# Eight of the row-layout heads moved to a key layout with split exponentials

## The chip, the cores and the metric

The kernel runs on one core of a Trainium2 chip. The core has a matrix engine (PE, with its weight loads shown apart as PEld), a vector engine (DVE), a scalar engine (ACT), a general engine (POOL) and a queue engine (SP) that here issues nearly all DMAs. Sixteen DMA engines serve all queues. Each engine takes its own instructions strictly in the order in which they stand; between engines there are only semaphores. The metric is the device time of one execution in microseconds.

## The reference

Two parts follow each other. The attention part hashes queries and keys into buckets, lets a query see only the keys of its own bucket, and takes a softmax over them. The second part mixes the attended rows over positions and gates them.

```python
def _attn_ref(q, k, v, proj):                 # q, k, v: 4 x 8 x 768 x 64
    q_bits = (np.einsum('bhsd,dk->bhsk', q, proj) > 0)   # 6 bits per row
    k_bits = (np.einsum('bhsd,dk->bhsk', k, proj) > 0)
    mask = q_bucket[:, :, :, None] == k_bucket[:, :, None, :]
    scores = np.where(mask, scale * np.matmul(q, k.transpose(0, 1, 3, 2)), -1e9)
    attn = np.exp(scores - np.max(scores, axis=-1, keepdims=True))
    attn = attn / (np.sum(attn, axis=-1, keepdims=True) + 1e-9)
    return np.matmul(attn, v)

def _moe_ref(x, w_in, w_spatial, b_spatial, w_out):      # x: 4 x 768 x 512
    h = np.maximum(x @ w_in, 0.0)                        # 1024 wide: u, v
    v_n = (v - mean(v)) / np.sqrt(var(v) + 1e-6)
    v_s = np.einsum('ts,bsd->btd', w_spatial, v_n) + b_spatial[None, :, None]
    return (u * v_s) @ w_out
```

## The kernel before

There are 32 heads (4 batches of 8), two to a pair, and each head is worked in 6 steps of 128 rows. A step is named g = 6n + i for head n and tile i. Every large product is done in 16-bit pieces: a number is split into a high and a low half and three of the four partial products are summed.

**Row layout** (head 0 and heads 8 to 31, function `scores`). Step i takes 128 queries as rows and all 768 keys as columns. PE makes the scores in a PSUM tile `sp` by four matmuls (lines 291 and 292). DVE reads `sp` and takes the row minimum of the negated scores into `nb` (line 293, it also writes a throw-away tile `jk`, and a small second instruction reads the accumulated value out). ACT reads `sp` again and makes the exponentials `ex` with `nb` as bias (line 295). ACT casts them to 16 bit, the high half of `pp` (line 298). DVE subtracts to get the low half (line 299); for tile 2, and for tiles 0 and 3 of heads below 16, POOL does that. The product with V needs the keys on the partitions, so SP issues a DMA transpose `pt<-pp` of both halves (line 301). Five steps later (`LAG`), `weighted` multiplies `pt` with the halves of V by 18 small matmuls (lines 314 to 316).

**Key layout** (heads 1 to 7, set `KEYS`). Step i takes 128 keys as rows and all queries as columns, so exponentials come out with the keys on the partitions and no transpose is needed. A row maximum cannot be taken there, so it is made first: `row_max` computes the masked scores of 128 queries by two matmuls into a tile `mp` (line 241), DVE reduces it (line 243), and after the sixth tile the maxima are cast (line 248), transposed by PE (line 251), copied (line 253) and written by a small DMA on SP as one more row into the operand `ab` (line 254). `scores_k` then makes scores that have the maximum in them already (lines 262 and 263), and ACT makes the exponentials as 32-bit numbers (line 265), which `weighted_k` multiplies three steps later (`LAGK`) with the 32-bit V (line 275). The row maxima of head n are made one per step from g = 6n - 10 to 6n - 5 (`LEAD`).

**Buffers.** `sp` and `mp` share two PSUM buffers (`ps_sc`). `ex` has 3 buffers, `pp` 3 (`PB`), and `pt` 5 (`PTB`); the 32-bit exponentials of the key layout take `pt` buffers too.

**What stands beside it.** Loads, the splitting of q and k (`hl`) and the building of `ab` for head n + 2 go along with the steps. The gating part of a batch is 28 units of 12 or 18 matmuls each (lines 361, 402, 417, 432), handed out at 28 units per 48 steps once the last pair of the batch is done, so that it fills PE while the next batch's heads run; the units of the last batch come after the last head. A scheduler orders each engine's instructions by a priority (`at(g, k)`) and its own estimate of readiness; the order is fixed when the program is built.

SP's queue is in order too: a transpose that waits for its `pp`, or for a `pt` buffer that `weighted` has yet to give back, holds up every load behind it.

## Time and profile before

| | us |
|---|---|
| median of 3 runs | 736.97 |
| runs | 735.91, 736.97, 740.86 |
| span of the profiled execution | 741.7 |
| from the start to the first exponential of head 8 | 174.9 |
| heads 8 to 31 | 174.9 to 655 |
| what is left of the gating part | 655 to 741.7 |

The page gives no other time for the profiled execution than its span; the span is 4.7 us over the median of the runs and 0.8 us over the highest. In the tables below, an idle time "<- X" is time in which the engine stood still until X released it. Busy times of PE have modelled ends, so they are an upper bound of what PE does.

### The profile page before, as it was taken

Reading aid. Unit: us, or ns where it says so; the run is one execution under the profiler, and the core shown is the slowest. Engines: PE = TensorE matmul, PEld = TensorE weight load, DVE = VectorE, ACT = ScalarE, POOL = GpSimd, SP = SyncE. Lnnn points to the kernel's source line nnn. Section 1 sums busy time; section 2 is a strip of 40 time slices with the busy share of each in tenths; the row PEclk is TensorE's granted clock in tenths of the full one; section 3 lists DMA queues with packets and bytes.
Section 4 is the critical chain, followed back from the end, with each engine's and each line's share of the span. In section 5 each row is a group of like instructions: output and inputs, shape, how many; then the busy total and the mean of one; then the engine's idle time right before and its main releaser. Section 6 shows DMA issues by size and latency. Waiting matters only on the chain.

```text
span 741.7 us, 14927 instructions
## 1 busy us (share of the span) xinstructions
PE 631.5 (85%) x5759; PEld 400.4 (54%) x5759; DVE 520.6 (70%) x945; ACT 434.8 (59%) x668; POOL 321.2 (43%) x324
## 2 busy tenths in 40 slices
PE   1569898998988776997898899889898998999997
PEld 0237686776445444554544555556455565654553
DVE  4677795536799999567689798678698987755200
ACT  1344574346788676655676577667677776743221
POOL 5122443123458675264314565156235571451503
PEclk9768797999999989898999999999999999999999
DMA  9565554324999989996999799999999999860011
GB/s 235 149 123 155 133 148 102 99 55 97 224 237 197 215 207 187 213 178 138 234 202 199 138 210 213 211 211 212 206 210 181 194 175 213 182 136 15 1 42 43
DMA packets 290011, 120.95 MB, mean 163 GB/s; under 512 B 270740, under 2 KB 273812, under 8 KB 289940
## 3 DMA queue, kind: packets, MB, share of 16 engines
q1 hardware_dynamic: 287636, 119.11, 76.4%
q10 hardware_dynamic: 2304, 0.89, 0.5%
q8 instruction: 45, 0.74, 0.4%
q14 instruction: 26, 0.21, 0.1%
HBM read 28.33 MB, written 6.29 MB: 47 GB/s over the span
## 4 chain that ended last, share of the span: by engine, by line
PE 43%; DMA 21%; DVE 13%; issue 8%; ACT 6%; POOL 6%; SPq 3%; ACTq 0%; DVEq 0%; POOLq 0%
DMA pt<-pp 14%; PE pv L275 6%; PE vps L361 6%; PE ops L432 5%; PE sps L417 5%; PE ups L402 5%; DMA ab<-hl 4%; PE sp L291 3%; DVE jk L293 3%; PE sp L292 3%; DVE pp L299 2%; PE sp L262 2%; PE pv L314 2%; ACT ex L295 2%; PE sp L263 2%
## 5 line engine op out<-in xcount | busy, mean ns | idle before, releaser
L295 ACT ACTIVATE ex<-sp,nb 128x768 f32<-128x768 f32 x150 | 134.1, 897 | 54.8 <-DVE jk L293 48.9
L299 DVE TENSOR_TENSOR pp<-ex,pp 128x768 f16<-128x768 f32 x116 | 126.2, 1089 | 47.6 <-ACT pp L298 46.5
L293 DVE TENSOR_SCALAR_CACHE_REDUCE jk<-sp 128x768 bf16<-128x768 f32 x150 | 142.4, 949 | 24.1 <-PE sp L292 22.2
L298 ACT CAST pp<-ex 128x768 f16<-128x768 f32 x150 | 124.3, 829 | 50.0 <-DMA pt<-pp 43.9
L314 PE MATMUL pv<-vp,pt 128*128 128x65 f16 x900 | 108.2, 198 | 40.5 <-DMA pt<-pp 40.2
L291 PE MATMUL sp<-ab 128*128 128x384 f16 x300 | 103.2, 344 | 31.6 <-ACT ex L295 19.3
L314 PEld LDWEIGHTS <-pt 128*128 128x128 f16 x900 | 86.7, 101 | 67.2 <-DMA pt<-pp 53.4
L299 POOL TENSOR_TENSOR pp<-ex,pp 128x768 f16<-128x768 f32 x34 | 58.1, 1708 | 131.1 <-ACT pp L298 124.6
L315 PE MATMUL pv<-vp,pt 128*128 128x64 f16 x900 | 108.0, 197 | 0.0
L316 PE MATMUL pv<-vp,pt 128*128 128x65 f16 x900 | 107.8, 198 | 0.0
L292 PE MATMUL sp<-ab 127*128 127x384 f16 x300 | 103.9, 346 | 0.0
L417 PE MATMUL sps<-ws,vn 128*128 128x384 f16 x576 | 100.9, 329 | 1.5 <-DVE sg L180 1.0
L315 PEld LDWEIGHTS <-pt 128*128 128x128 f16 x900 | 87.0, 100 | 11.3 <-issue 1.3
L316 PEld LDWEIGHTS <-pt 128*128 128x128 f16 x900 | 86.9, 100 | 3.1 <-issue 0.5
L417 PEld LDWEIGHTS <-vn 128*128 128x128 f16 x576 | 55.3, 99 | 37.8 <-issue 3.9
L432 PE MATMUL ops<-wo,g 128*128 128x512 f16 x288 | 70.9, 391 | 1.5 <-ACT o L436 0.9
L275 PEld LDWEIGHTS pv<-vf,ex 128*128 128x128 f32 x504 | 68.5, 208 | 4.1 <-issue 1.6
L402 PE MATMUL ups<-xt,wi 128*128 128x384 f16 x384 | 69.1, 333 | 1.3 <-ACT u L405 0.9
L361 PE MATMUL vps<-wi,xt 128*128 128x512 f16 x288 | 68.0, 383 | 1.4 <-DMA xt<-xs 1.3
L275 PE MATMUL pv<-vf,ex 128*128 128x65 f32 x504 | 67.0, 286 | 0.0
L333 POOL TENSOR_TENSOR x<-x,xf 128x384 f32<-128x384 f32 x32 | 35.5, 1110 | 64.1 <-DVE x L332 64.1
L422 POOL TENSOR_TENSOR sy<-sy,u 128x384 f32<-128x384 f32 x32 | 36.6, 1145 | 49.3 <-DVE sy L421 49.2
(87 smaller groups left out, 1010.7 us busy)
## 6 DMA issues: line engine op xcount, KB each, us to landing
qk<-kq SPq DMA_DIRECT2D x16, 768.0 KB
ab<-hl SPq DMA_DIRECT2D x31, 384.0 KB
ab<-hl SPq DMA_DIRECT2D x34, 192.0 KB
out<-o SPq DMA_DIRECT2D x24, 256.0 KB
v<-v SPq DMA_DIRECT2D x13, 384.0 KB
raw<-w_in SPq DMA_DIRECT2D x16, 256.0 KB
pt<-pp SPq DMA_TRANSPOSE x150
raw<-w_sp SPq DMA_DIRECT2D x12, 192.0 KB
```

What stands on the lines that cost most here:

```text
L275: nc.tensor.matmul(acc[:, qi, :], lhsT=ex[:, qi * P:(qi + 1) * P], rhs=vf[p % 2][:, 2 * i + e, :], start=(i == 0 and qi == 0), stop=(i == ...
L291: nc.tensor.matmul(ps[:, c], lhsT=t[:, 0, qs], rhs=t[:, 1, cs], start=True, stop=False)
L292: nc.tensor.matmul(ps[:, c], lhsT=t[0:P - 1, 3, qs], rhs=t[0:P - 1, 2, cs], start=False, stop=True)
L293: nc.vector.tensor_scalar(jk, ps, -ISQ, None, op0=ALU.mult, op1=ALU.min, accum_out=nb)
L295: st["ex", n, i] = nc.scalar.activation(ex, ps, AF.Exp, bias=nb, scale=ISQ).ins
L298: nc.scalar.copy(pp[:, 0], ex)
L299: (nc.gpsimd if i in (PL_POOL if n >= 2 * NH else PL_POOL1) else nc.vector).tensor_tensor(out=pp[:, 1], in0=ex, in1=pp[:, 0], op=ALU.subtract)
L314: nc.tensor.matmul(acc, lhsT=pt[:, c, :], rhs=vh, start=(i == 0 and c == 0), stop=False)
L315: nc.tensor.matmul(acc[:, 0:D], lhsT=pt[:, c, :], rhs=vl, start=False, stop=False)
L316: nc.tensor.matmul(acc, lhsT=pt[:, NT + c, :], rhs=vh, start=False, stop=(i == NT - 1 and c == NT - 1))
L361: nc.tensor.matmul(ps, lhsT=xt[c][:, gx, i * P:(i + 1) * P], rhs=wi[gw][:, c, F2:DF], start=(k == 0), stop=(k == 3 * NPAIR - 1))
L417: nc.tensor.matmul(ps[:, :HS], lhsT=vn[gv][:, c, d * P:(d + 1) * P], rhs=ws[gw][:, c, hs], start=(k == 0), stop=(k == 3 * NT - 1))
```

## The change

Heads 10, 13, 16, 19, 22, 25, 28 and 31 leave the row layout. They get row maxima ahead of time like heads 1 to 7, and scores by `scores_k`. Unlike those, their exponentials are split into 16-bit halves by ACT and DVE, the halves lie in a `pt` buffer (tile `pk`), and `weighted_k` multiplies them with the 16-bit halves of V, again by 18 small matmuls. All six subtractions of such a head are DVE's, none is POOL's.

```diff
     def has_keys(p):
-        return 2 * p in KEYS or 2 * p + 1 in KEYS
+        return 2 * p in KF32 or 2 * p + 1 in KF32
...
@@ scores_k
+        if n in KSPLIT:
+            pp = wk.tile([P, 2, 2, HS], F16, tag="pt", bufs=PTB, name=f"pk{n}_{i}")
+            ex = wk.tile([P, 2, HS], F32, tag="ex", bufs=EB, name=f"ex{n}_{i}")
+            st["ex", n, i] = nc.scalar.activation(ex, ps, AF.Exp, scale=ISQ).ins
+            nc.scalar.copy(pp[:, 0], ex)
+            nc.vector.tensor_tensor(out=pp[:, 1], in0=ex, in1=pp[:, 0], op=ALU.subtract)
+            st["pt", n, i] = pp
+            return
...
@@ weighted_k
+        if n in KSPLIT:
+            pk = ex.rearrange("p g c q -> p g (c q)")
+            vl, vh = vp[p % 2][:, 2 * i + e, 0:D], vp[p % 2][:, 2 * i + e, D:2 * D + 1]
+            for qi in range(NT):
+                qs = slice(qi * P, (qi + 1) * P)
+                nc.tensor.matmul(acc[:, qi, :], lhsT=pk[:, 0, qs], rhs=vh, start=(i == 0 and qi == 0), stop=False)
+                nc.tensor.matmul(acc[:, qi, 0:D], lhsT=pk[:, 0, qs], rhs=vl, start=False, stop=False)
+                nc.tensor.matmul(acc[:, qi, :], lhsT=pk[:, 1, qs], rhs=vh, start=False, stop=(i == NT - 1 and qi == NT - 1))
+            return
...
-    KEYS = {1, 2, 3, 4, 5, 6, 7}
+    KF32 = {1, 2, 3, 4, 5, 6, 7}
+    KSPLIT = {10, 13, 16, 19, 22, 25, 28, 31}
+    KEYS = KF32 | KSPLIT
```

The order of instructions changes at two kinds of places. In the names below the first number after the letters is the head (of `hl`, `xs`, `xt`, `v32` and `qk`: the pair), the second the tile, the last one a serial number.

DVE, around the second step of head 18, before the change. `jk` is the minimum, `pp` the subtraction, the others belong to the gating part:

```order
L299 TENSOR_TENSOR pp18_0_4592<-ex18_0_4590,pp18_0_4592 128x768
L293 TENSOR_SCALAR jk18_1_4639,nb18_4582<-sp18_1_4640 128x768
L370 BN_AGGR mv1_0_4272<-bs1_2_4459 128x2
L339 TENSOR_TENSOR xs8_4525<-x16_4522,xs8_4525 128x6x64
L369 BN_STATS bs1_3_4544<-vr1_3_4541 128x6
L293 TENSOR_SCALAR jk18_2_4671,nb18_4582<-sp18_2_4672 128x768
L377 TENSOR_SCALAR ve1_0_4462<-mv1_0_4272 128x3
L370 BN_AGGR mv1_3_4543<-bs1_3_4544 128x2
L299 TENSOR_TENSOR pp18_1_4648<-ex18_1_4646,pp18_1_4648 128x768
```

The same engine at the same place now; `mx19` are reductions for head 19, which is one of the eight:

```order
L243 TENSOR_REDUCE mx19_4444<-mp19_3_4601 128x1
L310 TENSOR_SCALAR jk18_0_4627,nb18_4626<-sp18_0_4628 128x768
L316 TENSOR_TENSOR pp17_5_4596<-ex17_5_4594,pp17_5_4596 128x768
L386 BN_STATS bs1_4_4684<-vr1_4_4682 128x6
L243 TENSOR_REDUCE mx19_4444<-mp19_4_4641 128x1
L405 TENSOR_SCALAR vy1_2_4546<-vr1_2_4525,mv1_0_4335,rs1_0_4532 128x512
L387 BN_AGGR mv1_3_4583<-bs1_4_4684 128x2
L310 TENSOR_SCALAR jk18_1_4687,nb18_4626<-sp18_1_4688 128x768
L316 TENSOR_TENSOR pp18_0_4636<-ex18_0_4634,pp18_0_4636 128x768
L243 TENSOR_REDUCE mx19_4444<-mp19_5_4701 128x1
```

Between two minima of heads 17 and 18 there now stands one more full-width reduction, and each `mp` that it reads takes one of the two PSUM buffers that the `sp` tiles use.

SP, from the end of head 18 through head 19, before the change:

```order
L344 DMA_TRANSPOSE xt8_4833<-xs8_4525 128x12x128
L301 DMA_TRANSPOSE pt18_5_4847<-pp18_5_4844 128x12x128
L301 DMA_TRANSPOSE pt19_0_4906<-pp19_0_4903 128x12x128
L211 DMA ab1_83<-hl10_4422 64x2x1536
L212 DMA ab1_83<-hl10_4422 64x1536
L301 DMA_TRANSPOSE pt19_1_4944<-pp19_1_4941 128x12x128
L158 DMA v32_11_4946<-v 128x768
L301 DMA_TRANSPOSE pt19_2_4992<-pp19_2_4989 128x12x128
L301 DMA_TRANSPOSE pt19_3_5033<-pp19_3_5030 128x12x128
L301 DMA_TRANSPOSE pt19_4_5083<-pp19_4_5080 128x12x128
L301 DMA_TRANSPOSE pt19_5_5155<-pp19_5_5152 128x12x128
L152 DMA qk12_5157<-kq 128x1536
```

SP now, from the second step of head 18 to the first of head 20:

```order
L318 DMA_TRANSPOSE pt18_1_4699<-pp18_1_4696 128x12x128
L254 DMA ab3_85<-mt19_4711 1x6x128
L361 DMA_TRANSPOSE xt8_4894<-xs8_4487 128x12x128
L318 DMA_TRANSPOSE pt18_2_4744<-pp18_2_4741 128x12x128
L318 DMA_TRANSPOSE pt18_3_4814<-pp18_3_4811 128x12x128
L318 DMA_TRANSPOSE pt18_4_4861<-pp18_4_4858 128x12x128
L158 DMA v32_11_4998<-v 128x768
L318 DMA_TRANSPOSE pt18_5_4908<-pp18_5_4905 128x12x128
L152 DMA qk12_5230<-kq 128x1536
L318 DMA_TRANSPOSE pt20_0_5263<-pp20_0_5260 128x12x128
```

Head 19's six transposes are gone, and the small write of its maxima (`ab3_85<-mt19`) stands among the transposes of head 18.

More of the change, by code (lines that the diff above doesn't have):

```diff
@@ L165, in has_keys @@
     def has_keys(p):
-        return 2 * p in KEYS or 2 * p + 1 in KEYS
+        return 2 * p in KF32 or 2 * p + 1 in KF32
     def has_queries(p):
-        return not (2 * p in KEYS and 2 * p + 1 in KEYS)
+        return not (2 * p in KF32 and 2 * p + 1 in KF32)
     def hash_rows(p):
@@ L327, in normalize @@
         rv = wk.tile([P, NT], F32, tag="rv", bufs=2, name=f"rv{n}")
-        nc.vector.tensor_scalar(rv, pv[:, :, D], 1e-9, 1.0 / SX if n in KEYS else SQ / SX, op0=ALU.add, op1=ALU.mult)
+        nc.vector.tensor_scalar(rv, pv[:, :, D], 1e-9, 1.0 / SX if n in KF32 else SQ / SX, op0=ALU.add, op1=ALU.mult)
         nc.vector.reciprocal(rv, rv)
```

## The prediction

> **What bounds the kernel now.** I read the page first, for the shares and the slices:
>
> ```profile
> PE 631.5 (85%) x5759; PEld 400.4 (54%) x5759; DVE 520.6 (70%) x945; ACT 434.8 (59%) x668; POOL 321.2 (43%) x324
> DMA  9565554324999989996999799999999999860011
> q1 hardware_dynamic: 287636, 119.11, 76.4%
> HBM read 28.33 MB, written 6.29 MB: 47 GB/s over the span
> PE 43%; DMA 21%; DVE 13%; issue 8%; ACT 6%; POOL 6%; SPq 3%; ACTq 0%; DVEq 0%; POOLq 0%
> ```
>
> No engine is full over the whole span, the DMA engines are full through the middle, and the chain that ended last (the fifth line) is PE for 43% and DMA for 21%. So the answer lies in the stages. The windows by stage come next; behind the times of the five engines stand the granted clock, the DMA share and GB/s:
>
> ```profile
> 174.90:210.20 35.30, 30.29 (x276) 17.37 (x275) 28.91 (x52) 27.94 (x43) 18.93 (x17) 0.95 0.99 198
> 210.20:297.40 87.20, 65.24 (x682) 40.46 (x680) 84.80 (x148) 65.46 (x112) 58.60 (x53) 0.92 0.97 205
> 297.40:490.20 192.80, 164.93 (x1708) 100.87 (x1706) 144.56 (x255) 124.36 (x180) 83.04 (x77) 0.95 0.96 194
> 490.20:655.00 164.80, 154.01 (x1654) 97.11 (x1652) 134.71 (x249) 117.06 (x167) 79.24 (x72) 0.98 1.00 195
> 655.00:741.70 86.70, 81.88 (x501) 43.93 (x498) 19.54 (x42) 22.26 (x44) 27.23 (x27) 0.99 0.13 42
> 349.40:638.60 289.20, 257.33 (x2740) 159.03 (x2739) 232.43 (x427) 200.13 (x288) 129.57 (x119) 0.97 1.00 200
> ```
>
> Columns after the length: PE, PEld, DVE, ACT, POOL. The first four rows are heads 8 to 31, 480.1 us, the only place that the change touches. The DMA share is 0.96 to 1.00 throughout. But PE is busy 414.5 of the 480.1 us, and 93% of the fourth row; and in the second row (heads 10 to 13) DVE is busy 84.8 of 87.2 us, 97%. The last row is 15 heads, 90 steps: a step lasts 3.21 us and takes 2.58 us of DVE and 2.86 us of PE. So three resources lie close together, and taking load off one can win little.
>
> Third, the waits, over 174.9 to 655 us (the first three rows) and within 210.2 to 297.4 us (the last two):
>
> ```profile
> ACT pp L298 <- DMA pt<-pp: 43.9, 33, 3.7
> PE pv L314 <- DMA pt<-pp: 34.5, 29, 4.0
> PE sp L291 <- ACT ex L295: 18.9, 15, 5.1
> PE pv L314 <- DMA pt<-pp: 12.6, 9, 4.0
> PE sp L291 <- ACT ex L295: 7.1, 6, 1.9
> ```
>
> PE stands still 34.5 us for transposes and 18.9 us for ACT, and ACT itself 43.9 us for the `pp` buffers that transposes still read. That is all a relieved DMA can give PE, and 12.6 + 7.1 us of it lie where DVE is full, so I count 21.9 and 11.8 us.
>
> **The change part by part.**
>
> *Transposes removed: 48.* One moves 128 x 1536 x 2 bytes = 0.393 MB. Queue q1 takes 76.4% of 741.7 us for 119.11 MB, 4.76 us a MB, so one transpose is 1.87 us of all DMA engines (an estimate from that row) and 48 are 90 us. The DMA work of the four rows falls from about 470 to 380 us, 79% of the time. How long a transpose waits under load the chain shows:
>
> ```profile
> 28.65 3.54 DMA pt<-pp
> 395.85 8.67 DMA pt<-pp
> ```
>
> 3.54 us early, where the DMA is half idle, 8.67 us in the full stretch. A third of the heads has no transposes, so a third of the 21.9 us goes, 7.3 us. Of the other 14.6 us, bounded by nothing and all, I take two thirds, 9.7 us, since 79% is nearer to the idle case. ACT's stall on `pp` is why `ex` is late; bounded by 0 and 11.8 us, I take half, 5.9 us. ACT then waits next for `jk`.
>
> *Clock.* The four rows lose (1 - clock) x length = 1.8 + 7.0 + 9.6 + 3.3 = 21.7 us of full PE speed. With fewer standstills I take 5 us of it, between 0 and 15.
>
> *Row maxima added: 8 x 6,* with two matmuls each, plus eight times the small operations. The rows, with those that leave:
>
> ```profile
> 461.18 0.33 PE L291 MATMUL sp<-ab 128*128 128x384 f16 x1
> 461.35 0.33 PE L292 MATMUL sp<-ab 127*128 127x384 f16 x1
> L251 PE MATMUL tp<-ident,m 128*6 128x128 f16 x7 | 1.6, 232 | 0.0
> L243 DVE TENSOR_REDUCE mx<-mp 128x1 f32<-128x768 f32 x42 | 39.8, 952 | 23.3 <-PE mp L241 23.2
> L248 DVE TENSOR_SCALAR m<-mx 128x6 f16<-128x6 f32 x7 | 2.6, 367 | 0.2
> L253 DVE COPY mt<-tp 6x128 f16<-6x128 f16 x7 | 1.4, 205 | 2.4 <-PE tp L251 2.4
> L293 DVE TENSOR_SCALAR_CACHE_REDUCE jk<-sp 128x768 bf16<-128x768 f32 x150 | 142.4, 949 | 24.1 <-PE sp L292 22.2
> L293 DVE DVE_READ_ACCUMULATOR jk<-sp 128x1 f32 x150 | 12.2, 81 | 0.0
> L299 DVE TENSOR_TENSOR pp<-ex,pp 128x768 f16<-128x768 f32 x116 | 126.2, 1089 | 47.6 <-ACT pp L298 46.5
> L299 POOL TENSOR_TENSOR pp<-ex,pp 128x768 f16<-128x768 f32 x34 | 58.1, 1708 | 131.1 <-ACT pp L298 124.6
> L295 ACT ACTIVATE ex<-sp,nb 128x768 f32<-128x768 f32 x150 | 134.1, 897 | 54.8 <-DVE jk L293 48.9
> L265 ACT ACTIVATE ex<-sp 128x768 f32<-128x768 f32 x42 | 33.9, 806 | 32.2 <-PE sp L263 28.9 <-PE mp L241 3.0
> ```
>
> Score matmuls of this width start 0.17 us apart, so one row maximum is 0.33 us of PE. Outside the DVE-bound stretch stand 42 of the 48 (all but head 13's): 42 x 0.333 + 7 x 0.232 = 15.6 us. PE is 93% busy in the fourth row, so I put all of it on the path.
>
> *DVE.* It gains 48 x 0.952 + 8 x (0.367 + 0.205) = 50.3 us and 10 subtractions that were POOL's (10.9 us), and loses 48 x (0.949 + 0.081) = 49.4 us: 11.8 us net. Where DVE is full that is time: heads 10 and 13 lose 12 minima (12.4 us) and take over four subtractions (4.4), heads 11 and 12 get head 13's maxima (5.7 + 0.6): -1.7 us. Elsewhere DVE is at 75 to 82% and the sum hides there, but not evenly: a step with a maximum takes 2.58 + 0.95 = 3.53 us of DVE. The ten subtractions off POOL cost nothing to lose, POOL being 43% busy.
>
> *The two PSUM buffers.* `mp` stands between consecutive `sp`, so PE can start the next scores only when ACT has read the last. The nearest rows are those of heads 1 to 7, which do this now, over the whole span:
>
> ```profile
> PE sp L262 <- ACT ex L265: 4.8, 5, 2.1
> PE mp L241 <- DVE mx L243: 4.5, 3, 3.0
> PE sp L291 <- DVE mx L243: 2.0, 2, 1.9
> ```
>
> 11.3 us over 42 maxima, 0.27 us each: 42 x 0.27 = 11.3 us. Below this the bound is nothing; above it stands a rival.
>
> *ACT.* 48 exponentials become 0.09 us shorter (806 for 897 ns); nothing, ACT is 59% busy. The cast of a split step writes into a `pt` buffer, so ACT now waits for PE's weighted sum of five steps before, with the next exponential behind it on ACT and PE behind that. Before, SP had that wait:
>
> ```profile
> SPq L301 <- PE pv L316: 57.0, 41, 3.2
> ```
>
> 1.39 us in 41 of 150 transposes; on 48 casts that would be 18 us. I take nothing, because a cast comes an exponential (0.81 us) after its scores and PE runs that weighted sum right behind those scores; 18 us is the other end.
>
> *SP and the tail.* SP loses 48 transposes and gets eight small writes among head n - 1's transposes; each stands behind DVE's copy, which runs ahead of the subtraction that the next transpose waits for, so nothing. The last head has no transpose at its end; PE is busy there (81.88 of 86.7 us), so nothing, with 3.5 us as the other end. The 18 weighted matmuls a step are the same in both layouts.
>
> **The sum** against the profiled execution: -7.3 - 9.7 - 5.9 - 5.0 - 1.7 + 15.6 + 11.3 = -2.7 us, from 741.7 to 739.0 us. The span lies 4.7 us over the median of 736.97, so as a median about 734 us.
>
> **One rule against it.** The DMA share as a proof of a full DMA is what a page doubts. The Trainium skill, Perfetto Trace Analysis, "Identifying the Most-Contended Engine", says to judge the DMA by the use of HBM and not by occupancy, since sixteen engines make occupancy misleading. By that rule, with 47 GB/s here, the DMA would not be the bound and its relief would give next to nothing; that case stands below as the last rival. The trace sides against it in part: PE's 34.5 us are waits for transposes.
>
> **The rivals.**
>
> *The DMA was the real brake (faster).* All of the 21.9 + 11.8 us of standstill goes, the buffers cost nothing, clock and DVE as above: -33.7 - 5 - 1.7 + 15.6 = -24.8, a median of about 712 us. For it: 0.96 to 1.00 DMA share everywhere. Against it: PE would have to be busy 430 of 455 us, 94%, over all heads, which only the fourth row shows.
>
> *The shared PSUM buffers become the brake (slower).* From scores to the next scores it is then four matmuls (0.66), `jk` (1.03), `ex` (0.90), 2.6 us, and 4.5 us if each read finds one instruction ahead (a subtraction, 1.09; a cast, 0.83). Against 3.21 us that is +1.29 a step where I counted 0.60. If this holds in half of the 42 steps it adds 14.5 us: 749 us; in all, 763. It decides from 15 steps on (15 x 0.69 = 10 us). For it: 3.53 us of DVE in such a step, so `jk` will often find DVE taken. Against it: heads 1 to 7 pay 0.27 us. The Trainium skill, Perfetto Trace Analysis, "Identifying Performance Opportunities", says that a gap that keeps coming back on the engine that should be full can mean too few buffers for the next tile; the 18.9 us of `sp <- ex` agree with that even now.
>
> *Transposes do not bind (slower).* Then only the third of the waits goes: -7.3 - 1.7 + 15.6 + 11.3 = +17.9, 755 us.
>
> **How the numbers follow.** About 1% (7.4 us) is what a measurement of this kernel can tell from no change. Forecast (gains and costs cancel) 0.40, of which 0.05 falls beyond 1% on the fast side and 0.03 on the slow side; DMA the brake 0.33, all faster; shared buffers 0.21, with 0.03 of it within 1%; transposes not binding 0.06, slower. Faster 0.38, same 0.35, slower 0.27. The forecast's own range is 722 to 746 us, since its unknown terms (two thirds, half, 5 us) move some 12 us either way. The whole range, 710 to 752 us, leaves out the better half of the first rival's spread and the worse half of the last two, about 0.2.
>
> **What would show it.** Right: DMA share near 0.8 in heads 8 to 31, PE's wait for `pt` from 34.5 to about 17 us, its waits for `ex` and `mx` there up by some 5 us net, PE busy near 430 us, DVE still full in heads 10 to 13. First rival: waits for `pt` and `ex` both under 10 us. Second: `sp <- ex` and `mp <- mx` over 30 us together and steps with maxima near 4 us. Third: the wait for `pt` still above 25 us with the DMA share at 0.8. I would be wrong altogether if ACT's casts waited for PE's weighted sums by many microseconds, or if DVE in heads 10 to 13 grew.

## The result

The changed kernel takes 787.2 us (median of 4 runs, 782.8 to 792.0) where the kernel before, beside it on the same chip, takes 736.4 us (733.9 to 740.9): a ratio of 1.069, 95% interval [1.063, 1.075]. It is slower by 51 us. The forecast was 734 us, so it was wrong on the side, and the range of 710 to 752 did not hold the time. Three executions of the kernels further below ran at a lower granted clock and over 1.5% above the fastest of their kernel; the medians and ranges given hold them, and without them the kernel with later maxima takes 775.0 us and the two with three score buffers 807.8 and 826.1 us.

The page of the changed kernel shows first what the change was made for: the queue of the transposes took 76.4% of the span before and takes 58.3% now, and the slices of the DMA are no longer full. Yet the span grew, and the share of the DMA in the chain that ended last fell (21% to 16%) while PE's and DVE's rose:

```profile
span 787.1 us, 14951 instructions
...
PE 661.9 (84%) x5863; PEld 412.5 (52%) x5863; DVE 527.3 (67%) x923; ACT 434.1 (55%) x668; POOL 305.3 (39%) x322
...
DMA  9675452317877594767659359579676764701011
...
q1 hardware_dynamic: 212468, 100.24, 58.3%
...
PE 46%; DVE 16%; DMA 16%; ACT 9%; issue 7%; SPq 3%; POOL 2%; ACTq 1%; DVEq 0%; POOLq 0%
...
L243 DVE TENSOR_REDUCE mx<-mp 128x1 f32<-128x768 f32 x90 | 85.3, 950 | 29.4 <-PE mp L241 29.3
```

The waits of the changed kernel between 172 and 690 us (engine, line, what released it; total us, times, longest):

```profile
ACT ex L312 <- DVE jk L310: 78.2, 56, 3.7
...
PE pv L331 <- DMA pt<-pp: 38.7, 26, 4.1
DVE jk L310 <- PE sp L309: 34.0, 27, 8.4
...
PE sp L308 <- DVE mx L243: 9.6, 10, 1.6
...
PE mp L241 <- DVE mx L243: 8.0, 8, 3.5
...
PE sp L308 <- ACT ex L312: 7.8, 9, 2.0
...
ACT pp L315 <- DMA pt<-pp: 5.1, 4, 2.8
```

ACT's wait for transposes is nearly gone (43.9 to 5.1 us). PE's is not: 38.7 us, where 34.5 was and 17 was forecast. But 30.9 us of it, counted in the trace, lie in the 48 steps in which a row maximum of a split head now stands (9.5 us in the same steps before), and the DMA share, ahead of the GB/s in the window of these heads, is 0.70 where it was 0.96 to 1.00:

```profile
172.00:682.00 510.00, 427.98 (x4218) 257.27 (x4217) 388.97 (x664) 321.33 (x482) 215.78 (x207) 0.91 0.70 147
```

And two waits grew that belong to the scores: ACT waits 78.2 us for DVE's minimum and DVE 34.0 us for PE's scores. Over the same stretch these were, before:

```profile
ACT ex L295 <- DVE jk L293: 34.7, 33, 3.1
...
DVE jk L293 <- PE sp L292: 17.7, 20, 4.7
```

The scores are late, then, and the engines behind them starve. Where, the starts of the exponentials tell. I took the mean length of a step (from one exponential to the next) in heads 8 to 31 of both traces, by what else is done in it:

| steps | before, us | after, us | sum of the difference |
|---|---|---|---|
| 48 with a row maximum of a split head | 3.46 | 5.05 | +76 |
| 47 of the split heads | 3.18 | 2.83 | -16 |
| 48 others | 3.37 | 3.09 | -13.5 |

Up to head 8 and after the start of the last head the two traces agree to about 2 us. So the other steps gain 30 us, and the steps with row maxima take that back two and a half times. They do not take it evenly. With the six steps counted by how far they stand ahead of their split head (n is the split head; the maxima stand at steps 6n - 10 to 6n - 5):

```
step        -10   -9   -8   -7   -6   -5      (us, mean over the eight split heads)
before     3.15 3.89 4.30 2.76 4.04 2.62
after      8.00 6.55 3.92 3.80 3.90 4.10
```

The steps of the first two maxima last 2.5 and 1.7 times as long as before. One such place, from the timeline of the changed kernel, the steps around the first maximum for head 19. ACT first (start, us, engine, line, operation):

```profile
382.20 0.90 ACT L312 ACTIVATE ex<-sp,nb 128x768 f32<-128x768 f32 x1 [0.51 <-DVE xs L356]
...
385.01 0.90 ACT L312 ACTIVATE ex<-sp,nb 128x768 f32<-128x768 f32 x1 [1.05 <-DVE jk L310]
...
393.98 0.90 ACT L312 ACTIVATE ex<-sp,nb 128x768 f32<-128x768 f32 x1 [1.63 <-DVE jk L310]
```

PE's scores and maxima in the same 9 us, without the weighted sums and gating units between them:

```profile
383.64 0.33 PE L309 MATMUL sp<-ab 127*128 127x384 f16 x1
...
388.17 0.85 PE L175 MATMUL hp<-qk,hc 128*32 128x384 f32 x8
...
391.56 0.33 PE L241 MATMUL mp<-ab 127*128 127x384 f16 x1
...
391.72 0.33 PE L308 MATMUL sp<-ab 128*128 128x384 f16 x1
```

And SP's queue:

```profile
383.71 1.46 SPq L318 DMA_TRANSPOSE pt<-pp  x1
385.22 0.64 SPq L211 DMA_DIRECT2D ab<-hl  x1
385.90 0.60 SPq L212 DMA_DIRECT2D ab<-hl  x1
386.96 2.43 SPq L318 DMA_TRANSPOSE pt<-pp  x1
```

The exponential that ends at 385.9 frees a score buffer. The next scores start at 391.7, right behind the first matmul of `mp`. That matmul needs the operand of head 19, and the two transfers that bring it (lines 211 and 212) are issued at 385.2 and 385.9, because SP has them behind the transpose of the step. The kernel itself ties them there: in a head of the row layout `build` stands under `tc.issue_after(st["tr"])`, the transpose of the step, and in a head of the key layout it is not. PE is not idle meanwhile; the planner has put other matmuls there. Before the change nobody needed that operand for another ten steps.

### The profile page after: what moved, and what is told of

The parts are those of the page before. It is cut to its first block, busy times and chain, and to the rows that moved or that the text cites. A ratio compares the mean times of both kernels' runs of the same rounds, so it can differ in the third digit from the quotient of the medians.

```text
span 787.1 us, 14951 instructions
## 1 busy us (share of the span) xinstructions
PE 661.9 (84%) x5863; PEld 412.5 (52%) x5863; DVE 527.3 (67%) x923; ACT 434.1 (55%) x668; POOL 305.3 (39%) x322
## 3 DMA queue, kind: packets, MB, share of 16 engines
q1 hardware_dynamic: 212468, 100.24, 58.3%
## 4 chain that ended last, share of the span: by engine, by line
PE 46%; DVE 16%; DMA 16%; ACT 9%; issue 7%; SPq 3%; POOL 2%; ACTq 1%; DVEq 0%; POOLq 0%
DMA pt<-pp 10%; PE sps L434 6%; PE ops L449 6%; PE vps L378 5%; PE pv L292 5%; PE ups L419 5%; DVE jk L310 4%; PE sp L262 3%; PE sp L263 3%; DMA ab<-hl 3%; DVE mx L243 3%; PE sp L308 2%; PE sp L309 2%; ACT ex L312 2%; DVE pp L316 2%
## 5 line engine op out<-in xcount | busy, mean ns | idle before, releaser
L312 ACT ACTIVATE ex<-sp,nb 128x768 f32<-128x768 f32 x102 | 91.7, 899 | 95.3 <-DVE jk L310 92.1
L310 DVE TENSOR_SCALAR_CACHE_REDUCE jk<-sp 128x768 bf16<-128x768 f32 x102 | 96.9, 950 | 38.6 <-PE sp L309 37.9
L331 PE MATMUL pv<-vp,pt 128*128 128x65 f16 x612 | 81.2, 202 | 43.9 <-DMA pt<-pp 43.8
L243 DVE TENSOR_REDUCE mx<-mp 128x1 f32<-128x768 f32 x90 | 85.3, 950 | 29.4 <-PE mp L241 29.3
L308 PE MATMUL sp<-ab 128*128 128x384 f16 x204 | 75.9, 372 | 28.4 <-DVE mx L243 11.6
L316 DVE TENSOR_TENSOR pp<-ex,pp 128x768 f16<-128x768 f32 x78 | 82.4, 1056 | 24.6 <-ACT pp L315 21.9
L331 PEld LDWEIGHTS <-pt 128*128 128x128 f16 x612 | 61.1, 104 | 66.5 <-DMA pt<-pp 58.9
L315 ACT CAST pp<-ex 128x768 f16<-128x768 f32 x102 | 84.5, 830 | 15.8 <-DMA pt<-pp 5.1
L333 PE MATMUL pv<-vp,pt 128*128 128x65 f16 x612 | 80.8, 203 | 0.0
L309 PE MATMUL sp<-ab 127*128 127x384 f16 x204 | 76.8, 377 | 0.0
L262 PE MATMUL sp<-ab 128*128 128x384 f16 x180 | 61.7, 343 | 8.8 <-ACT ex L312 4.4
L241 PE MATMUL mp<-ab 127*128 127x384 f16 x180 | 55.4, 388 | 14.1 <-DVE mx L243 12.6
```

The source lines that it names most:

```text
L243: nc.vector.reduce_max(st["mx", n][:, i:i + 1], ps, axis=AX.XY)
L308: nc.tensor.matmul(ps[:, c], lhsT=t[:, 0, qs], rhs=t[:, 1, cs], start=True, stop=False)
L309: nc.tensor.matmul(ps[:, c], lhsT=t[0:P - 1, 3, qs], rhs=t[0:P - 1, 2, cs], start=False, stop=True)
L310: nc.vector.tensor_scalar(jk, ps, -ISQ, None, op0=ALU.mult, op1=ALU.min, accum_out=nb)
L312: st["ex", n, i] = nc.scalar.activation(ex, ps, AF.Exp, bias=nb, scale=ISQ).ins
L316: (nc.gpsimd if i in (PL_POOL if n >= 2 * NH else PL_POOL1) else nc.vector).tensor_tensor(out=pp[:, 1], in0=ex, in1=pp[:, 0], op=ALU.subtract)
```

## The experiments

Four theories: the shared score buffers, by the chain of reads that the second rival priced; the order that the planner makes of the lost buffer on PE; the late arrival of the operands that the build's transfers bring; and the plain work, DVE's 48 reductions and PE's 96 matmuls. The kernel before ran beside each of the five groups of runs, with medians of 738.4, 736.4, 736.6, 738.4 and 739.5 us, so medians of different groups can be subtracted to about 3 us.

### Taking the row maxima apart

**No row maxima.**

```diff
-    rml = [(NT * n + i - NT - LEAD, n, i) for n in sorted(KEYS) for i in range(NT)]
+    rml = [(NT * n + i - NT - LEAD, n, i) for n in sorted(KF32) for i in range(NT)]
...
+                nc.gpsimd.memset(nb, 0.0)
```

> Leaves out the row maxima of the eight split heads: their 96 matmuls, 48 reductions, eight transposed copies and eight small transfers; their exponentials get a bias of zero. Everything else of the change stays, so the time shows what the removed transposes and the shorter split steps are worth alone. If the cost lies in the row maxima in any of its forms (shared buffers, place in the order, DVE load, PE work): the 76 us that the 48 steps with maxima grew by go, and the 30 us won in the other steps stay: about 705 us, 697 to 715. If the transposes did not bind (rival): no gain is left, 730 to 740. If the split steps themselves carry the loss: still over 770.

711.8 us (707.9 to 713.5), 0.964 of before, [0.957, 0.971]: 26.6 us faster than before. Its waits between 172 and 680 us, and the window of heads 8 to 30 (PE, PEld, DVE, ACT, POOL, clock, DMA share, GB/s):

```profile
PE pv L334 <- DMA pt<-pp: 18.4, 14, 2.6
...
ACT pp L318 <- DMA pt<-pp: 14.0, 13, 2.5
```

```profile
172.00:606.00 434.00, 391.38 (x4123) 241.78 (x4123) 342.80 (x602) 317.31 (x482) 215.55 (x207) 0.95 0.83 173
```

PE's wait for transposes is halved, as forecast. What the change removes is worth 26.6 us; what the row maxima cost is 787.2 - 711.8 = 75.4 us. The 26.6 us are not the transposes' alone, though: with the 48 transposes 48 minima have left DVE, which is busy 480.9 us here and 520.6 us before:

```profile
PE 624.7 (88%) x5759; PEld 396.8 (56%) x5759; DVE 480.9 (68%) x859; ACT 429.1 (60%) x668; POOL 306.3 (43%) x322
```

**DVE's reductions alone.**

```diff
-            nc.tensor.matmul(ps[:, c], lhsT=t[0:P - 1, 3, i * P:(i + 1) * P],
-                             rhs=t[0:P - 1, 2, c * HS:(c + 1) * HS], start=True, stop=True)
-        nc.vector.reduce_max(st["mx", n][:, i:i + 1], ps, axis=AX.XY)
+            nc.vector.reduce_max(st["mx", n][:, i:i + 1], bt, axis=AX.X)
```

> Leaves out the 96 matmuls of the row maxima of the split heads; DVE does 48 reductions of the same 768 columns on a constant tile in SBUF instead, and all that follows the maximum stays. Theory of the shared ring: no score loses its buffer, 710 to 730 us. Theory of DVE's load: 770 to 790. Theory of PE's work alone (96 x 0.33 = 32 us): 745 to 760.

738.6 us (732.8 to 743.7): 26.8 us more than without maxima. It lies between the ranges of the theories: DVE's work is not the whole of the cost, and no trifle either. 48 reductions of 0.95 us are 45.6 us, and 26.8 of them reach the end.

The same run bears on the transposes. It has 48 fewer of them than the kernel before, and DVE is as busy as before (526.9 and 520.6 us); yet it takes the time of before, 1.001 of it [0.997, 1.006]:

```profile
PE 631.7 (86%) x5767; PEld 399.4 (54%) x5767; DVE 526.9 (71%) x923; ACT 430.3 (58%) x668; POOL 308.2 (42%) x322
...
PE pv L334 <- DMA pt<-pp: 24.0, 23, 3.1
```

So without relief for DVE the missing transposes won nothing, with the reductions placed as here. How the 26.6 us divide between transposes and minima no run shows.

**The matmuls with a short reduction, and the place in the buffers alone.** The first keeps both matmuls of 384 columns and reduces 16 columns; the second also cuts each matmul to 8 columns.

```diff
-        nc.vector.reduce_max(st["mx", n][:, i:i + 1], ps, axis=AX.XY)
+            nc.vector.reduce_max(st["mx", n][:, i:i + 1], ps[:, :, 0:8], axis=AX.XY)
...
-                             rhs=t[0:P - 1, 2, c * HS:(c + 1) * HS], start=True, stop=True)
+                             rhs=t[0:P - 1, 2, c * HS:c * HS + 8], start=True, stop=True)
```

> The 96 matmuls stay and write into the ring of the scores as in the change, but DVE reduces only 16 of the 768 columns, some 0.1 us in place of 0.95, so the maxima are no bounds (they are taken as at least zero). Theory of the shared ring: each score still finds its buffer taken by the one before it, so most of the loss stays: 760 to 780 us. Theory of DVE's load: 48 x 0.85 = 41 us and the waits behind it go, 715 to 740. Theory of the place in the order: the first two steps with maxima stay at 6 to 8 us, 760 to 785.

> As e4_short, but of each row maximum of a split head only 2 x 8 of the 768 columns are multiplied (so also the PE work is left out, and the maxima are no bounds, taken as at least zero). What stays is the place that the maximum takes in the ring of two score buffers, and with it the order that the planner gives PE: 53 and 41 other matmuls behind the score tiles ten and nine steps ahead of the split head, where the kernel without maxima has 21 and 10. Theory of the ring and its order: the first two steps stay at 6 to 8 us and the run at 740 to 760. Theory of PE's work (96 x 0.33 = 32 us of the 49 that e4_short cost): 715 to 730.

760.5 us (756.3 to 763.2) and 763.8 us (758.6 to 768.6), in the first range of the theory of the ring for the one and 4 us above it for the other. PE's 32 us of matmuls cost nothing that can be measured. A place in the ring of score buffers, with next to no work in it, costs 763.8 - 711.8 = 52.0 us. The parts add up: 711.8 + 26.8 + 52.0 - 3.3 = 787.3 us, and the change measures 787.2. That they meet to 0.1 us is chance: such differences are good to about 3 us, and 26.8 and 52.0 both hold the small operations behind the maxima, an estimated 6.4 us of PE and DVE by the prediction's rows (8 x (0.23 + 0.37 + 0.20)). The granted clock is not what costs: it is 0.91 in the change's window, but 0.95 in that of the kernel with the short reduction, which has the same long steps (7.98 and 6.33 us).

By steps, the two costs lie like this:

```
step (us, means)       -10    -9   -8 to -5
no row maxima         3.23  3.03  3.14
DVE's reductions      2.88  4.74  3.70
place in the buffers  7.29  5.58  3.11
the change            8.00  6.55  3.93
```

The place costs (7.29 + 5.58 - 6.26) x 8 = 53 us in the first two steps and nothing in the four behind them, though these share the buffers just as much. That is against the chain of reads as the price of the place, which would show in all six. The reductions' cost does not lie evenly either: the step at -9 lasts 4.74 us and the one at -6 lasts 6.33, the other four 2.3 to 3.2. Why it falls there is not shown.

**The row maxima in the gating units' ring.**

```diff
+            for c in range(2):
+                ps = ps_m.tile([P, 512], F32, tag=MT, name=f"mp{n}_{i}_{c}")
...
+                nc.vector.reduce_max(mh[:, c:c + 1], ps[:, :HS], axis=AX.X)
```

> The row maxima of the split heads go, in two halves of one bank each, through the ring of the gating units (two buffers), with two half reductions and a tensor_max of two columns; the ring of the scores is left to the scores. Nothing is left out. Theory of the shared ring: steps with maxima come back from 5.05 us to about 3.7 us, the run to 715 to 730 us. Theory of the place in the order (maxima wait for the build's transfers and hold PE's order): still 760 to 790, the first two steps with maxima still 6 to 8 us. Theory of DVE's load (48 x 0.95 us plus the new small operations): 775 to 795.

810.7 us (805.9 to 813.8), beyond all three ranges. The steps with maxima came back as it said (3.35 us in the mean, 3.49 and 3.22 at -10 and -9). But the half tiles queue up with the gating units, and the last are ready too late: the step into a split head lasts 15.2 us. For head 19 PE's timeline shows it, with `tp` as the transposition of the finished maxima:

```profile
426.87 0.33 PE L271 MATMUL sp<-ab 128*128 128x384 f16 x1
...
427.46 0.33 PE L243 MATMUL mp<-ab 127*128 127x384 f16 x1
...
429.43 0.32 PE L243 MATMUL mp<-ab 127*128 127x384 f16 x1 [0.45 <-ACT vr L391]
...
432.29 0.22 PE L260 MATMUL tp<-ident,m 128*6 128x128 f16 x1
...
438.68 0.33 PE L272 MATMUL sp<-ab 128*128 128x384 f16 x1
```

The second score matmul of the head, which reads the row of the maxima, comes 6.4 us after `tp`. The loss moved; it did not go.

### Moving the row maxima in time

**Two steps later.**

```diff
+    rml = [(NT * n + i - NT - (2 if n in KSPLIT else LEAD), n, i) for n in sorted(KEYS) for i in range(NT)]
```

> The row maxima of split heads come two steps later (eight to three steps ahead of their head); nothing is left out. Theory of the ring and its order: the long steps move along, to eight, seven and six steps ahead (51, 48 and 41 other matmuls there), ten and nine are normal at 3 to 4 us, and the run stays at 780 to 805. Theory of the build (the first maxima wait for the operands that the build's transfers bring, two steps before): the excess goes, 735 to 755.

777.2 us (774.8 to 786.6), some 3 us under the range of the theory of the order and far above that of the build. The long steps moved along (6.46 and 5.41 us at -8 and -7; 3.45 and 3.76 at -10 and -9), as the theory of the order said, and the run gained only 10 us. The first maximum now starts 1.9 us after the buffer is free (6.9 in the change), so the operands are no longer what it waits for, for the most part, and yet steps stay long.

**In two bursts of three.**

```diff
+    rml = [(NT * n + (3 * (i // 3) + 1 if n in KSPLIT else i) - NT - LEAD, n, i) for n in sorted(KEYS) for i in range(NT)]
```

> The six row maxima of a split head come in two bursts of three, at the steps nine and six ahead, in place of one in each of six steps; nothing is left out, and PE and DVE do the same work. The planner's order then has one long stretch (70 other matmuls behind the score tile nine steps ahead) in place of two (55 and 46). Theory of the ring and its order: the loss goes down with the number of steps in which the score's second buffer is taken, 750 to 772. Theory of the work (DVE 48 x 0.95, PE 96 x 0.33, wherever it lies): as the change, 780 to 795.

774.7 us (774.0 to 776.2), between the theories' ranges: 12.5 us gained, one step of 10.4 us at -9 and one of 6.4 at -6.

### Forcing PE's order

The planner's order has 55 and 46 other matmuls (means over the eight, in the order as built; the records of the trace give 55 and 43) behind the score tiles at -10 and -9, where the kernel without maxima has 21 and 10. **Tying** puts the weighted sums and gating units of a step behind its score tile:

```diff
+            st["sp"] = nc.tensor.matmul(ps[:, c], lhsT=t[0:P - 1, 3, qs], rhs=t[0:P - 1, 2, cs], start=False, stop=True).ins
...
+        if n < N and any(0 <= g - (NT * (h - 1) - LEAD) <= NT for h in KSPLIT):
+            tie.enter_context(tc.issue_after(st["sp"]))
         while wv < N * NT and wv + (LAGK if wv // NT in KEYS else LAG) <= g:
```

> The change with nothing left out, all its work and its two shared score buffers; only in the steps with row maxima of split heads (and one behind) PE's weighted sums and gating units of a step are tied behind that step's score tile in PE's order. Behind the score tiles ten and nine steps ahead there are then 40 and 16 other matmuls (55 and 46 in the change, 21 and 10 without maxima). Theory of the order (the planner, finding no free score buffer, pulls later work ahead of the score): the 49 us of the ring go for the most part and DVE's 27 stay: 735 to 755 us. Theory of the ring itself (each score waits for the exponential of the one before it, whatever the order): no gain, 775 to 795.

> As e7_dummy (a place in the ring of score buffers per row maximum of a split head, 2 x 8 columns of work; maxima taken as at least zero, no bounds), and as in e9_tied PE's later work tied behind the score tile in those steps: 38 and 16 other matmuls ten and nine steps ahead where e7_dummy has 53 and 41. What the place costs is 763.8 - 711.8 = 52 us. If what the tie saves and what DVE's reductions cost are independent: 763.8 - 16 = 748 us, 741 to 755. If the order is all of it and DVE's reductions kept e9_tied long: 715 to 735. If the tie only helped DVE's queue: 757 to 770.

771.2 us (767.0 to 777.9) with all the work, 752.9 us (752.0 to 754.5) with the place alone: 16 and 11 us back, of 52. The first is in neither range, the second is what independent parts would give. The first long step hardly changed (7.73 us at -10 with all the work, 5.49 at -9). PE's waits of e9_tied between 172 and 690 us show what came in place of the other work:

```profile
PE sp L308 <- ACT ex L312: 22.3, 15, 4.4
PE mp L241 <- DMA ab<-hl: 16.3, 5, 6.7
PE sp L308 <- DVE mx L243: 14.4, 11, 2.7
...
PE pv L331 <- DMA pt<-pp: 3.8, 4, 1.2
```

With less work to put in front, PE waits for the score buffers, mostly in the steps from -8 on, and in five heads at -10 for the build's transfers. As a control the kernel before, with the tie in every step from head 8 on, where e9_tied has it around the maxima alone:

> The kernel before, without split heads, with the same tie in every step from head 8 on: a control. If the tie helps only where a row maximum takes a score's buffer: within 1% of before, 730 to 743. If the order of before loses time in the same way: 715 to 730.

749.2 us (747.7 to 749.7), 1.017 [1.013, 1.021] of before: neither expectation. The tie costs some 13 us there, so it has a price of its own and is no clean removal of an order.

**Tying and holding units back** takes away the rest of what stood ahead of the scores (18 and 3 other matmuls):

```diff
-            while queue and credit >= 1.0:
+            while queue and credit >= 1.0 and not any(-14 <= g - NT * h <= -9 for h in KSPLIT):
```

> As e9_tied (all the work of the change, two shared score buffers, later work tied behind the score tile), and gating units are held back from 14 to nine steps ahead of a split head and made up for behind. PE's order then has 18 and 3 other matmuls behind the score tiles ten and nine steps ahead (55 and 46 in the change, 40 and 16 in e9_tied, 21 and 10 without maxima), while the scores still wait for the exponential of the step before. Theory of the order: the two long steps go to 4 us or less and the run to 735 to 757 us (the 738.6 with DVE's reductions alone, and what held-back units cost later). Theory of the wait for the buffer: 762 to 790, the two steps stay over 5.5 us.

> The same tie and the same holding back on e7_tied (a place in the ring per row maximum, 2 x 8 columns of work; the maxima are no bounds, taken as at least zero). Theory of the order: the 41 us that e7_tied still lost against the run without maxima (752.9 - 711.8) go for the most part, 712 to 732 us. Theory of the wait for the buffer: 745 to 760.

801.8 us (800.0 to 804.5) and 784.4 us (783.2 to 785.4): both slower than without the holding, by 31 us, and beyond both theories as written. The 31 us do not lie at the first two maxima: with all the work the steps at -10 and -9 last 9.37 and 4.78 us, together 0.9 us more than with the tie alone, while the four behind them, where the held-back units are made up for, last 5.07 us in place of 3.76. But with the other work gone from in front of it, PE now stands still at the first maximum. The waits between 172 and 690 us, of e14_hold and then of e14_dummy:

```profile
PE mp L241 <- DMA ab<-hl: 51.3, 7, 8.0
```

```profile
PE mp L242 <- DMA ab<-hl: 43.8, 6, 7.8
```

Seven and six of the eight heads, 7.3 us each: PE waits for the build's transfers, and the scores are queued behind the waiting matmul; their buffer has been free for 3.7 to 6.2 us when it starts. In the change no such wait is among the page's rows, because other matmuls stand there, and the step is as long. With the tie alone the wait was 16.3 us in five heads (above). The sizes of the transfers, from the page's list of DMA issues:

```profile
ab<-hl SPq DMA_DIRECT2D x31, 384.0 KB
ab<-hl SPq DMA_DIRECT2D x34, 192.0 KB
```

I took the times of these issues and of the first `mp` matmul from the traces, as means over the split heads, in us:

```
                        issue of the first `hl` transfer   first mp after   first mp after the
                        after the exponential of 6n - 12   that issue       buffer came free
the change                        5.2                          5.2               6.9
place alone (e7_dummy)            5.4                          5.0               8.0
e14_dummy                         5.2                          4.2               6.7
two steps later (e5_lead2)        6.1                          5.4               1.9
block 8 to 15, heads 10 to 15   -17.0                         22.0               1.9
block 24 to 31, heads 24, 25      4.5                          5.7               7.2
block 24 to 31, heads 26 to 31  -17.1                         22.6               2.2
```

In e14_dummy the middle number lies between 3.9 and 4.4 us for all eight heads, which is what a landing looks like. In the change it is 4.1 to 8.3: the first maximum starts soon after its operand is there, or later. In heads 2 to 7, whose rate the prediction used, the same transfers go out 17.7 us ahead of that exponential's end, and the first maximum stands 24.3 us behind them. The Trainium skill, TensorE: Matmul & The Clock Gate, "Part 3: Packing small matmuls — row/col tiling", says that matmuls are strictly first in, first out with no reordering; the waiting `mp` with ready scores behind it agrees with that.

### Blocks

**Heads 8 to 15, and heads 24 to 31,** split in one block:

```diff
-    KSPLIT = {10, 13, 16, 19, 22, 25, 28, 31}
+    KSPLIT = {8, 9, 10, 11, 12, 13, 14, 15}
```

> The eight split heads are heads 8 to 15 in one block in place of every third from 10 on; nothing is left out and the sum of the work is that of the change. All but a few of the row maxima then fall into heads by key layout, whose scores need no negative maximum on DVE ahead of the exponential, so the chain from a score to the next in the same buffer is 0.66 + 0.90 us in place of 0.66 + 1.03 + 0.90. Theory of the ring: the loss shrinks, 735 to 765. Theory of the work alone: 780 to 795. Transposes saved in heads 8 to 15 alone, and heads 16 to 31 as before: the gain is at most what the 48 transposes gave in the run without maxima, 26 us, so not under 712.

> The eight split heads are heads 24 to 31 in one block, nothing left out. Theory of the ring: like the block 8 to 15 (733.6 us), since again all but a few maxima fall into heads whose scores need no negative maximum ahead of the exponential: 725 to 745. If the block 8 to 15 was good only for its place (early, where gating units have hardly begun): 755 to 785.

733.6 us (725.8 to 736.1), 0.995 [0.991, 0.999] of before, and 771.9 us (769.0 to 775.0). The first came out under the range of the theory of the ring, the second far above it, where the expectation put a block that was good only for its place. What the two traces show is where their maxima fall. In a head by key layout SP has no transposes and the build no tie to one, and the build's transfers go out 17 us ahead of the exponential that they follow otherwise (table above). In the late block the maxima of heads 24 and 25 still fall into heads 22 and 23, whose scores have transposes: these two last 28.0 and 29.0 us (before 17.0 and 18.6), 21 us lost, while inside the block no head is like that. The rest of its loss is another one: from head 24 to the end it takes 243.8 us where before took 232.9. There the DMA share is 0.21 and PE is busy 121.4 of 130 us:

```profile
550.00:680.00 130.00, 121.40 (x1276) 75.68 (x1275) 105.15 (x162) 87.73 (x128) 47.42 (x49) 0.99 0.21 48
```

The early block takes 153.8 us for heads 8 to 15, where before took 174.5. Its entry costs 4.7 us (head 8 starts at 179.6 us, before at 174.9); heads 6 and 7 have no transposes. Another 7.6 us are lost in heads 16 to 30 and 1 us behind them, so 7.4 us of the 20.7 are left in the two profiled executions, and 2.8 us between the medians.

**The early block tied, and a longer one** (heads 8 to 19), with the tie from head 8 on:

```diff
-    KSPLIT = {10, 13, 16, 19, 22, 25, 28, 31}
+    KSPLIT = set(range(8, 20))
...
+        if n < N and g >= 8 * NT:
+            tie.enter_context(tc.issue_after(st["sp"]))
```

> The split heads in one block, 8 to 15, as in e6_block8 (733.6 us), and PE's weighted sums and gating units tied behind the score tile in every step from head 8 on. Nothing is left out. Theory of the order: some of the block's maxima still cost by order, so 715 to 730. Theory of the ring itself: as e6_block8, 728 to 738.

> Split heads 8 to 19 in one block with PE's later work tied behind the score tile from head 8 on; twelve split heads in place of eight, nothing left out. Theory that removed transposes pay as long as maxima fall into heads by key layout: each further head as the first eight (7 us gained by eight), 722 to 729. Theory that PE then binds (94% busy in the block 8 to 15, and 35% busier heads by key layout add its row maxima): no further gain, 729 to 742.

729.5 us (726.9 to 736.1), 0.992 [0.989, 0.995] of before: the best here of those that leave nothing out, faster than the kernel before by less than 1%. It lies in the ranges of both theories and, at 4 us from the block without the tie, does not decide between them. Twelve heads give 737.6 us (733.9 to 742.4), no gain any more, with PE busy 212.9 of 228 us and the DMA at a third:

```profile
172.00:400.00 228.00, 212.89 (x2161) 132.77 (x2161) 191.06 (x302) 150.56 (x224) 88.55 (x93) 0.99 0.34 83
```

### Three score buffers

The edit is the same for the change and for its control, which has DVE's reductions alone:

```diff
-    PSB = (2,2,2)
+    PSB = (3,1,1)
```

> The change with nothing left out, with three double-bank buffers for scores and maxima, taken from the weighted sums and the gating units, which keep one buffer each in place of two; that costs by itself, which the next kernel shows. Theory that the score's wait for its own buffer is the cost: this kernel less the next one is 0 to 20 us where the change less the same control was 49 (787.2 - 738.6). Theory of the planner's order (which here still puts 54 and 87 other matmuls behind the score tiles eleven and ten steps ahead, 20 and 18 in the control): the difference is 35 us or more.

> Control to e13_ring3: three score buffers and one each for weighted sums and gating units, and as in e3_dve_only no matmuls of row maxima for split heads (left out), with 48 reductions of the same width over a constant tile on DVE. With two buffers each this took 738.6 us. One buffer less for the gating units makes each wait for the reading of the one before it: 745 to 800 us. The theories differ on the difference to e13_ring3 alone.

808.1 us (799.2 to 816.0) and 831.1 us (823.9 to 839.3). The kernel with maxima is some 20 us faster than the one without, outside every expectation. One buffer each for weighted sums and gating units makes both kernels far slower than with two (787.2 and 738.6 us), so the pair compares two other kernels. It decides nothing.

## Why the prediction was wrong

**What the removed work is worth: about right in size, its source not separated.** For a kernel without maxima the prediction's terms are -7.3 - 9.7 - 5.9 - 5.0 and, for DVE in the full stretch without head 13's maxima, -12.4 + 4.4 = -8.0: -35.9 us in all, and -26.6 us is measured. PE's wait for `pt` went from 34.5 to 18.4 us (about 17 forecast), the DMA share to 0.83 (about 0.8). The 5 us of the clock did not come: 0.95 in that window, as over heads 8 to 31 before. The transposes were taken for the source of the gain, but 48 minima left with them, and where reductions keep DVE as busy as before nothing is won (738.6 for 738.4 us). The rule that was weighed against it (the Trainium skill, Perfetto Trace Analysis, "Identifying the Most-Contended Engine", judge the DMA by HBM use, then find which DMA resource binds; HBM use was 47 GB/s) was taken to mean next to no gain from the relief. PE's 16.1 us less of waiting for `pt` speak against that, the 738.6 us for it; no run decides. The third rival's sign, a wait for `pt` above 25 us, did come in the change (38.7 us), but mostly in the steps that the row maxima lengthened.

**"The two PSUM buffers", 42 x 0.27 = 11.3 us: the step that failed.** The place in the buffers costs 52.0 us, and it costs them in the first two steps of each six. The rate came from PE's waits in heads 1 to 7, as the nearest rows, and those heads differ: they have no transposes, so the operand of a row maximum is issued 17.7 us ahead of the point that it follows by 5.2 us in the split heads; and no gating units stand beside them that the planner could put ahead of the scores. From head 10 on the first maximum stands two steps behind its build, whose transfers SP issues behind a transpose, and which take some 4 us to land. `mp` then holds one of the two buffers and PE's place ahead of the next scores. The prediction walked through SP's queue for what the change adds to it, but not for what the change newly needs from it: a transfer that had twelve steps to spare had two. Nor could a rate of waits hold the planner's part: PE is idle 1.4 us in the 8.0 us of the step at -10 (mean of the eight, from the trace), the rest is filled with matmuls, most of them not of scores or maxima.

**"DVE", -1.7 us: mis-sized.** The 48 reductions alone cost 26.8 us. That DVE is at 75 to 82% outside the full stretch did not hide them. The text named a reason, 3.53 us of DVE in a step with a maximum, and did not price it; but the time lies at -9 and -6 and not in every such step, so that this is the reason is not shown. In the four later steps nearly the whole cost comes with the reductions: 3.93 us in the change, 3.70 with the reductions alone, 3.11 with the place alone and 3.14 without either.

**"Row maxima added", PE's 15.6 us: not there.** Full matmuls measured 3.3 us less than matmuls of 8 columns, within the runs' spread. PE busy at 93% in one row did not put added matmuls on the path.

**ACT's casts behind weighted sums: right.** They were costed at nothing, and the page of after has 2.5 us of such waits.

**The second rival** had the right place and the right sign, at 763 us, but not the mechanism. It priced a chain of reads in every step, to about 4 us. The later four steps last that (3.93 us), but the reductions alone bring them to 3.70, so some 0.2 us a step is left for the chain. Its sign did not come in the change: PE's waits `sp <- ex` and `mp <- mx` are 7.8 and 8.0 us in the rows above, not 30 together, while PE had other work in front. With that work tied, `sp <- ex` is 22.3 us and `sp <- mx` 14.4 us, so these waits are not absent from the kernel, and are covered in the change.

What stays open is how the 52 us divide between the late operand and the planner's order. Both lie in the same two steps and cover each other. Moving the maxima away from the landing gave 10 us, tying the order 16, and holding units back as well laid the landing bare. The two together (later maxima with the tie), and issuing the build ahead of the transposes, were not tried. That the late operand by itself holds PE is shown by its waits of 51.3 and 43.8 us; that the 52 us go without it is not shown. With the operand in time and the order as it was (two steps later) the steps stay long, and in the blocks, where the cost does go, the scores also need no minimum.

## What to carry to other kernels

When work is moved ahead in time, ask for each operand when it now arrives: follow the transfer that brings it back through its queue, not only the engine that computes. A price taken from other rows of the same kernel holds only where what feeds them is the same; here heads 1 to 7 had the same instructions, but their transfers were not tied behind a transpose and no gating units stood beside them. When a change removes work from two engines at once, put the load of one back before the gain is given to the other. And an idle time that the page does not show may be filled by a planner: a wait for the operand appeared on PE only when the work in front of it was taken away.

## What the runs showed of the hardware that was not expected

A transfer of 384 KB and one of 192 KB, issued one after the other, let the matmul that needs them start 3.9 to 4.4 us after the first issue. The Trainium skill, DMA: Bandwidth & Descriptors, "Anatomy of one DMA — SWDGE (gpsimd) path", gives, for another path of issue, 2.0 us plus the bytes at 436 GB/s: 2.9 us for the first alone as an estimate; the measured pair takes 1.0 to 1.5 us more, with the second issued 0.7 us behind the first. The granted clock did not rise with the relief: 0.95 over heads 8 to 30 in the kernel without maxima, as over heads 8 to 31 before.
